# A decode attention block: a stretch of unrolled head groups put into a hardware loop with fixed tiles and register-addressed loads

## The chip, the cores and the metric

The kernel runs on one core of one Trainium2 chip. The metric is the device time of one execution in microseconds (us); several executions are timed and medians quoted. An execution under the profiler gives a span about 2 us below the timed value, since it leaves out start and end.

Names: PE is the matmul engine, DVE the vector engine, ACT the scalar engine, SP the engine that here issues nearly all DMA loads. "SPq" in a profile line is SP's instruction queue. A load is one DMA instruction; it is spread over 16 DMA engines and is done, "landed", when all 16 have reported to its semaphore (16 landing records for each load in the traces).

## The reference, cut to what matters

```python
# x (4,1,512); k_cache, v_cache (4,32,4096,128) bf16; 32 heads of 128
h = layernorm(x) * (1 + ca) + sa
q = h @ wq                                          # per head
p = softmax(einsum('bhqd,bhkd->bhqk', q, k_cache) * 128**-0.5)
o = einsum('bhqk,bhkd->bhqd', p, v_cache)
x = x + ga * (o.reshape(...) @ wo)
# ... then a small gated MLP on 4 tokens
```

Only one query token per batch row is there, so K and V (134 MB each) are read once and nearly nothing else matters: 282.7 MB are read in all.

## The kernel before

Heads are taken in 8 groups of 4, and for each of the 4 batch rows one group is a "quad": 32 quads, each with one K load and one V load of 4 MB (128 partitions of 32 KB). Everything is unrolled by Python. `kt` and `vt` are double buffers handed out by a pool.

```python
def load(cache, i, tag, parts):
    t = kvp.tile([P, NT * DH], BF16, name=tag, bufs=2)
    a = 0
    for part in parts:
        b = a + NT * DH // part
        nc.sync.dma_start(out=t[:, a:b], in_=kv_view(cache, i)[:, a:b])
        a = b
    return t.rearrange("p (n d) -> p n d", d=DH)
# ... cut ...
st["k", 0] = load_k(0)
for i in range(NQ):                        # 32 quads
    if i + 1 < NQ:
        st["k", i + 1] = load_k(i + 1)
    if quads[i][1] == 0:                   # first quad of a group
        g = quads[i][0]
        if g < G - 1:
            st["wo", g] = wk.tile([P, NH, D], BF16, name="wo_g", bufs=2)
            nc.sync.dma_start(out=st["wo", g], in_=wo_w[g])
    st["v", i] = load_v(i)
    # ... cut: the last quad's extra loads and its order of work ...
    if i > 1: diagonal(i - 2)
    scores(i, 0)                           # DVE product, then 16 PE matmuls
    if i > 1: project(i - 2)
    scores(i, 1)
    fold(i, 0); fold(i, 1)
    if i != NQ - 2: softmax(i)
    if i > 0: values(i - 1)
    if i > 1: apply(i - 2)
```

Each load reports to one of eight semaphores, taken in turn over the whole program; before a semaphore is used again, SP waits until its last load has landed.

Of the kernel before, what the change touches and what calls it, by code (L numbers as in the profile page):

```python
# [16 lines left out]
def kernel(  # L17
# [16 lines left out]
    nc = tc.nc  # L34
# [35 lines left out]
    def vslot(cols):  # L70
        return kvp.tile([P, cols], BF16, name="vt", bufs=2)

    wm = vslot(J * 6 * D)
# [3 lines left out]
    wq = vslot(J * G * GW)  # L77
# [3 lines left out]
    quads = [(g, b) for g in range(G) for b in range(B)]  # L81

    def kv_view(cache, i):
        g, b = quads[i]
        return cache[b, g * NH:(g + 1) * NH].rearrange("h (s n) d -> (h s) (n d)", s=R)

    def load(cache, i, tag, parts):
        t = kvp.tile([P, NT * DH], BF16, name=tag, bufs=2)
        a = 0
        for part in parts:  # L90
            b = a + NT * DH // part
            nc.sync.dma_start(out=t[:, a:b], in_=kv_view(cache, i)[:, a:b])  # L92
            a = b
        return t.rearrange("p (n d) -> p n d", d=DH)

    def load_k(i):
        return load(A_k_cache, i, "kt", (2, 2) if i == len(quads) - 1 else (1,))

    def load_v(i):
        return load(A_v_cache, i, "vt", (2, 4, 8, 16, 16) if i == len(quads) - 1 else (1,))  # L100

    NQ = len(quads)
# [30 lines left out]
    NB = 3  # L133
# [135 lines left out]
    with tc.tile_pool(name="psum_att", bufs=1, space=bass.MemoryType.PSUM) as psum:  # L269
        st = {}  # L270

        def scores(i, half):
            g, b = quads[i]
            kt = st["k", i][:, half * HT:(half + 1) * HT, :]
            q = qbc[:, b, g, :]
            nc.vector.tensor_tensor(  # L276
                out=kt, in0=kt, in1=q[:, None, :].to_broadcast([P, HT, DH]), op=ALU.mult,
            )
            ps = psum.tile([P, HT, DC], F32, name="s_ps", bufs=2)
            for cc in range(DH // DC):  # L280
                nc.tensor.matmul(  # L281
                    ps, lhsT=ident, rhs=kt[:, :, cc * DC:(cc + 1) * DC],
                    start=(cc == 0), stop=(cc == DH // DC - 1),
                )
            st["s", i, half] = ps

        def fold(i, half):
            if half == 0:
                st["S", i] = wk.tile([P, NT], F32, name="S", bufs=3)
            nc.vector.tensor_reduce(  # L290
                out=st["S", i][:, half * HT:(half + 1) * HT], in_=st.pop(("s", i, half)),
                axis=AX.X, op=ALU.add,
            )

        def softmax(i):
            S = st.pop(("S", i))
            mx, P4 = mxs[i % NB], P4s[i % NB]
            nc.vector.tensor_reduce(out=mx[:, 0:1], in_=S, axis=AX.X, op=ALU.max)
            mT = wk.tile([P, R], F32, name="mT", bufs=2)
            nc.vector.transpose(out=mT, in_=mx)  # L300
            hm = wk.tile([P, 1], F32, name="hm", bufs=2)
            nc.vector.tensor_reduce(out=hm, in_=mT, axis=AX.X, op=ALU.max)
            hb = wk.tile([P, R], F32, name="hb", bufs=2)
# [3 lines left out]
            nm = wk.tile([P, R], F32, name="nm", bufs=2)  # L307
            nc.vector.transpose(out=nm, in_=hb)  # L308
            E = wk.tile([P, NT], F32, name="E", bufs=2)
            rs = wk.tile([P, 1], F32, name="rs", bufs=2)  # L310
# [7 lines left out]
            rs4 = wk.tile([P, NH], F32, name="rs4", bufs=3)  # L318
            nc.vector.tensor_scalar_mul(out=rs4, in0=mask4, scalar1=rs)
            st["rs4", i] = rs4  # L320

        def zsum(i):
            zo = psum.tile([P, 2, NH], F32, name="zo_ps", bufs=2)
            st["z", i], st["o", i] = zo[:, 0], zo[:, 1]
            if i == NQ - 1:
                st["z", i] = psum_s.tile([P, NH], F32, name="small", bufs=1)
            nc.tensor.matmul(
                st["z", i], lhsT=ones_f, rhs=st.pop(("rs4", i)), start=True, stop=True,
            )

        def values(i):


            P4 = P4s[i % NB]
            zsum(i)
            po = psum_s.tile([P, 4, DH], F32, name="big", bufs=2)
            NU = NT // 16
            for u in range(NU):
                for t in range(4):
# [3 lines left out]
                        rhs=st["v", i][:, n0:n0 + 4, :],  # L343
                        start=(u == 0), stop=(u == NU - 1), tile_position=(0, 32 * t),
                    )
            osb = wk.tile([P, 4, DH], F32, name="osb", bufs=2)
            nc.scalar.copy(out=osb, in_=po)  # L347
            st["osb", i] = osb

        def diagonal(i):  # L350

            osb = st.pop(("osb", i))
            for n in range(4):
                nc.tensor.matmul(  # L354
                    st["o", i], lhsT=osb[:, n, :], rhs=sel[:, NH * n:NH * n + NH],
                    start=(n == 0), stop=(n == 3),
                )

        def values_last(i):
            P4 = P4s[i % NB]  # L360
            zsum(i)
            for n in range(NT):
                nc.tensor.matmul(  # L363
                    st["o", i], lhsT=st["v", i][:, n, :], rhs=P4[:, n, :],
# [3 lines left out]
        def project(i):  # L368
            g, b = quads[i]
            if b == 0:  # L370
                st["oT", g] = wk.tile([P, NH, B], BF16, name="oT", bufs=2)
            oT = st["oT", g]
            rz = wk.tile([P, NH], F32, name="rz", bufs=2)
            nc.vector.reciprocal(out=rz, in_=st.pop(("z", i)))
            nc.vector.tensor_tensor(  # L375
                out=oT[:, :, b], in0=st.pop(("o", i)), in1=rz, op=ALU.mult,
            )
            if i == NQ - 1:
                apply(i)

        def apply(i):
            g, b = quads[i]
            if b == B - 1:
                oT = st.pop(("oT", g))
                if g < G - 1:
                    wo_g = st.pop(("wo", g))

                    pp = psum_s.tile([P, NH, B], F32, name="small", bufs=1)
                    for r in range(NH):
                        for hl in range(NH):  # L390
                            nc.tensor.matmul(
                                pp[hl * R:(hl + 1) * R, r, :], lhsT=ident[:, r::NH],
                                rhs=oT[:, hl, :], start=True, stop=True,
                                tile_position=(0, hl * R),
                            )
                    oT = wk.tile([P, NH, B], BF16, name="oP", bufs=2)
                    nc.vector.tensor_copy(out=oT, in_=pp)  # L397
                for hl in range(NH):
                    for jo in range(J):
                        nc.tensor.matmul(  # L400
                            attn_ps[:, jo, :],
                            lhsT=(wo_g[:, hl] if g < G - 1 else wo_l[hl // 2][:, hl % 2])[
                                :, jo * P:(jo + 1) * P],
                            rhs=oT[:, hl, :],
                            start=(g == 0 and hl == 0 and jo == 0),
                            stop=(g == G - 1 and hl == NH - 1),
                            skip_group_check=True,
                        )

# [19 lines left out]
        for i in range(NQ):  # L429
            if i + 1 < NQ:  # L430
                st["k", i + 1] = load_k(i + 1)
# [144 lines left out]
```

## Time and profile before

| | |
|---|---|
| time | 667.5 us |
| SP's loads: share of the 16 DMA engines' span | 98.9% |
| PE, DVE busy | 62%, 61% |
| one 4 MB load: 8 packets of 32 KB per engine, 1.213 us each (packet records) | 9.7 us |
| K load from issue to landing, median | 26.0 us |

These lines are from the page of the kernel before: its busy table, the DMA row (busy tenths in 40 equal slices of the span) and what the DMA engines moved in each slice (GB/s), the queue table (packets, MB, share of 16 engines; q1 is SP's queue, q8 is listed there as `instruction`, read here as instruction fetches), the chain of waits by engine, one group of instructions and two groups of loads.

```profile
span 665.5 us, 6939 instructions
PE 415.7 (62%) x3024; PEld 204.6 (31%) x3024; DVE 402.6 (61%) x475; ACT 41.3 (6%) x115; POOL 4.7 (1%) x21
...
DMA  9999999999999999999999999999999999999995
GB/s 379 439 425 427 437 439 424 429 438 434 427 428 441 428 428 434 435 426 434 433 436 424 436 435 430 423 439 435 428 431 435 433 430 432 437 426 435 428 417 236
...
q1 hardware_dynamic: 12640, 282.73, 98.9%
q8 instruction: 23, 0.38, 0.2%
...
DMA 62%; PE 24%; DVE 12%; issue 0%; SPq 0%; ACT 0%; DVEq 0%
...
L276 DVE TENSOR_TENSOR kt<-kt,qbc 128x8192 bf16<-128x8192 bf16 x64 | 282.7, 4420 | 82.9 <-DMA kt<-in_A_k_cache_dram 82.9
...
kt<-in_A_k_cache_dram SPq DMA_DIRECT2D x31, 4096.0 KB, 26.0
vt<-in_A_v_cache_dram SPq DMA_DIRECT2D x31, 4096.0 KB, 33.7
```

The DMA engines are full in every slice but the last. A K load moves for 9.7 us and takes 26 us to land, so about 16 us of other loads stand ahead of it. The chain seems to give PE and DVE a third, but that is only the path by which a K load's issue is reached; the engines that move bytes never stop. So a few us of delay at SP, PE or DVE should cost nothing, as long as these 16 us of queue don't run empty.

### The profile page before, as it was taken

To read this page: it belongs to the slowest core of one execution; us is meant where nothing else is said; L and a number is where in the kernel's file an instruction comes from. 1 tells how busy PE (TensorE), PEld (TensorE's weight loads), DVE (VectorE), ACT (ScalarE), POOL (GpSimd) and SP (SyncE) were. 2 spreads that over 40 slices of the span, in tenths; PEclk is the share of its full clock that TensorE was granted. 3 is DMA by queue.
4 is the path that set the end of the run, shared out by engine and by line. 5 is a ranking of instruction groups with operands and counts; after the bars stand their busy time and mean duration, and the time that the engine had idled before them with its cause. 6 is when DMAs were issued, how large, how long until landed. Compare 5 with 4: busy or idle time off the path is not lost.

```text
span 665.5 us, 6939 instructions
## 1 busy us (share of the span) xinstructions
PE 415.7 (62%) x3024; PEld 204.6 (31%) x3024; DVE 402.6 (61%) x475; ACT 41.3 (6%) x115; POOL 4.7 (1%) x21
## 2 busy tenths in 40 slices
PE   2557776655677655676555477654657655657775
PEld 2223333222333322233222233232223322223334
DVE  2166776675556576547666456666555666655762
ACT  1200000000000000000000000000000000000002
POOL 2000000000000000000000000000000000000000
PEclk9977777668887667887667788676888766888795
DMA  9999999999999999999999999999999999999995
GB/s 379 439 425 427 437 439 424 429 438 434 427 428 441 428 428 434 435 426 434 433 436 424 436 435 430 423 439 435 428 431 435 433 430 432 437 426 435 428 417 236
DMA packets 12749, 283.17 MB, mean 426 GB/s; under 512 B 1448, under 2 KB 1968, under 8 KB 4016
## 3 DMA queue, kind: packets, MB, share of 16 engines
q1 hardware_dynamic: 12640, 282.73, 98.9%
q8 instruction: 23, 0.38, 0.2%
q14 instruction: 6, 0.05, 0.0%
q0 software_dynamic: 64, 0.00, 0.0%
q10 hardware_dynamic: 16, 0.01, 0.0%
HBM read 282.73 MB, written 0.00 MB: 425 GB/s over the span
## 4 chain that ended last, share of the span: by engine, by line
DMA 62%; PE 24%; DVE 12%; issue 0%; SPq 0%; ACT 0%; DVEq 0%
DMA kt<-in_A_k_cache_dram 58%; PE s_ps L281 24%; DVE kt L276 11%; DMA vt<-in_A_v_cache_dram 3%; DMA wout_437<-in_B_w_out_dram 1%; PE big L341 0%; DVE S L290 0%; ACT E L311 0%; SPq L92 0%; DVE P_1_109 L314 0%; DVE P_0_105 L314 0%; PE y_ps L522 0%; DVE nm L308 0%; DVE mT L300 0%; SPq L78 0%
## 5 line engine op out<-in xcount | busy, mean ns | idle before, releaser
L281 PE MATMUL s_ps<-kt,ident 128*128 128x512 bf16 x1024 | 293.5, 457 | 185.5 <-DVE kt L276 185.5
L276 DVE TENSOR_TENSOR kt<-kt,qbc 128x8192 bf16<-128x8192 bf16 x64 | 282.7, 4420 | 82.9 <-DMA kt<-in_A_k_cache_dram 82.9
L281 PEld LDWEIGHTS <-ident 128*128 128x128 bf16 x1024 | 116.4, 114 | 351.1 <-issue 229.8
L290 DVE TENSOR_REDUCE S<-s_ps 128x64 f32<-128x512 f32 x64 | 44.3, 692 | 125.5 <-PE s_ps L281 125.5
L354 PE MATMUL zo_ps<-sel,osb 128*128 128x4 f32 x248 | 33.2, 257 | 26.6 <-ACT osb L347 26.6
L311 ACT ACTIVATE E<-S,nm 128x128 f32<-128x128 f32 x32 | 12.8, 401 | 563.4 <-DVE nm L308 563.4
L354 PEld LDWEIGHTS zo_ps<-sel,osb 128*128 128x128 f32 x248 | 30.6, 194 | 38.4 <-ACT osb L347 38.4
L341 PE MATMUL big<-vt,P_0_105 128*32 128x512 bf16 x352 | 21.0, 380 | 1.5 <-DMA vt<-in_A_v_cache_dram 1.5
L341 PE MATMUL big<-vt,P_1_109 128*32 128x512 bf16 x320 | 19.1, 380 | 0.0
L341 PE MATMUL big<-vt,P_2_113 128*32 128x512 bf16 x320 | 19.1, 380 | 0.0
L347 ACT COPY osb<-big 128x512 f32<-128x512 f32 x31 | 17.6, 566 | 20.0 <-PE big L341 20.0
L215 PE MATMUL big<-vt,hbc 128*32 128x512 bf16 x128 | 9.6, 471 | 5.2 <-DMA vt<-in_A_wq_dram 5.2
L314 DVE TENSOR_TENSOR P_1_109<-E,mask_99 128x512 bf16<-128x512 f32 x11 | 7.6, 692 | 6.8 <-ACT E L311 6.8
L314 DVE TENSOR_TENSOR P_0_105<-E,mask_99 128x512 bf16<-128x512 f32 x11 | 7.6, 692 | 6.7 <-ACT E L311 6.7
L341 PEld LDWEIGHTS <-P_0_105 128*32 128x32 bf16 x352 | 8.4, 96 | 8.9 <-DMA vt<-in_A_v_cache_dram 1.6
L314 DVE TENSOR_TENSOR P_2_113<-E,mask_99 128x512 bf16<-128x512 f32 x10 | 6.9, 692 | 6.2 <-ACT E L311 6.2
L400 PE MATMUL attn_ps<-oP,wo_g 128*128 128x4 bf16 x112 | 3.8, 164 | 10.6 <-DVE oP L397 10.6
L341 PEld LDWEIGHTS <-P_1_109 128*32 128x32 bf16 x320 | 7.6, 96 | 6.7
L341 PEld LDWEIGHTS <-P_2_113 128*32 128x32 bf16 x320 | 7.6, 96 | 6.7
L375 DVE TENSOR_TENSOR oT<-zo_ps,rz 128x4 bf16<-128x4 f32 x32 | 5.4, 168 | 7.1 <-PE zo_ps L363 6.0
L215 PEld LDWEIGHTS <-hbc 128*32 128x32 bf16 x128 | 4.4, 114 | 10.3 <-issue 8.4
L308 DVE STREAM_TRANSPOSE nm<-hb 128x32 f32<-128x32 f32 x32 | 6.8, 212 | 1.1
(221 smaller groups left out, 131.1 us busy)
## 6 DMA issues: line engine op xcount, KB each, us to landing
kt<-in_A_k_cache_dram SPq DMA_DIRECT2D x31, 4096.0 KB, 26.0
vt<-in_A_v_cache_dram SPq DMA_DIRECT2D x31, 4096.0 KB, 33.7
vt<-in_A_wq_dram SPq DMA_DIRECT2D x1, 4096.0 KB, 20.4
kt<-in_A_k_cache_dram SPq DMA_DIRECT2D x2, 2048.0 KB, 24.8
wo_g<-in_A_wo_dram SPq DMA_DIRECT2D x7, 512.0 KB, 26.5
vt<-in_w_mod_dram SPq DMA_DIRECT2D x1, 3072.0 KB, 9.8
vt<-in_A_v_cache_dram SPq DMA_DIRECT2D x1, 2048.0 KB, 17.8
win_434<-in_B_w_in_dram SPq DMA_DIRECT2D x1, 1344.0 KB
```

Of the source, the lines that this page charges most:

```text
L215: nc.tensor.matmul(qp[hl * R:(hl + 1) * R, 0:n], lhsT=hbc[:, j, b, :], rhs=wv[:, g0:g0 + n, hl, :], start=(j == 0), stop=(j == J - 1), til ...
L276: nc.vector.tensor_tensor(out=kt, in0=kt, in1=q[:, None, :].to_broadcast([P, HT, DH]), op=ALU.mult,)
L281: nc.tensor.matmul(ps, lhsT=ident, rhs=kt[:, :, cc * DC:(cc + 1) * DC], start=(cc == 0), stop=(cc == DH // DC - 1),)
L290: nc.vector.tensor_reduce(out=st["S", i][:, half * HT:(half + 1) * HT], in_=st.pop(("s", i, half)), axis=AX.X, op=ALU.add,)
L308: nc.vector.transpose(out=nm, in_=hb)
L311: nc.scalar.activation(out=E, in_=S, func=AF.Exp, bias=nm[:, 0:1], scale=att_scale, accum_out=rs,)
L314: nc.vector.tensor_tensor(out=P4[:, 0:NT, :], in0=E[:, :, None].to_broadcast([P, NT, NH]), in1=mask4[:, None, :].to_broadcast([P, NT, NH]) ...
L341: nc.tensor.matmul(po[32 * t:32 * t + 32], lhsT=P4[:, n0:n0 + 8, :], rhs=st["v", i][:, n0:n0 + 4, :], start=(u == 0), stop=(u == NU - 1), ...
L347: nc.scalar.copy(out=osb, in_=po)
L354: nc.tensor.matmul(st["o", i], lhsT=osb[:, n, :], rhs=sel[:, NH * n:NH * n + NH], start=(n == 0), stop=(n == 3),)
L375: nc.vector.tensor_tensor(out=oT[:, :, b], in0=st.pop(("o", i)), in1=rz, op=ALU.mult,)
L400: nc.tensor.matmul(attn_ps[:, jo, :], lhsT=(wo_g[:, hl] if g < G - 1 else wo_l[hl // 2][:, hl % 2])[:, jo * P:(jo + 1) * P], rhs=oT[:, hl, :],
```

## The change

Its intent is a smaller program. (Two words for what follows: the jump from the end of a pass to its start is a back edge; a drain is a stretch in which SP's queue of loads runs empty.) Groups 1 to 6 run in a hardware loop, six passes of four quads; the first five quads and the last three stay unrolled. For that every buffer is one fixed tile, the softmax buffers are four, wo has one buffer in place of two, and K, V and wo addresses come from a register. The accumulator is cleared by one matmul so that all later ones accumulate.

```diff
+    kts = [kvp.tile([P, NT * DH], BF16, name=f"kt{a}", align_bytes=128) for a in range(2)]
+    vts = [kvp.tile([P, NT * DH], BF16, name=f"vt{a}", align_bytes=128) for a in range(2)]
 ... cut: all other buffers likewise ...
+    def kv_view(cache, g, b):
+        return cache[b, bass.ds(g * NH, NH)].rearrange("h (s n) d -> (h s) (n d)", s=R)
-    NB = 3
+    NB = 4
 ... cut ...
+        wo_g = wk.tile([P, NH, D], BF16, name="wo_g", align_bytes=128)
+            q = qbc[:, b, bass.ds(g, 1), :]
 ... cut ...
+        def step(g, b, first=9):
+            last = g is G - 1 and b == B - 1
+            if not last:
+                load(A_k_cache, kts[(b + 1) % 2], g + (b + 1) // B, (b + 1) % B,
+                     (2, 2) if g is G - 1 and b == B - 2 else (1,))
+            if b == 0 and first > 0:
+                nc.sync.dma_start(out=wo_g, in_=wo_w[bass.ds(g - 1, 1)])
+            load(A_v_cache, vts[b % 2], g, b, (2, 4, 8, 16, 16) if last else (1,))
 ... cut: the same order of work as before ...
+        load(A_k_cache, kts[0], 0, 0, (1,))
+        for i in range(B + 1):
+            step(i // B, i % B, i)
+        with tc.For_i(1, G - 1, 1, iteration_sync="reg_based") as g:
+            for b in range(1, B):
+                step(g, b)
+            step(g + 1, 0)
+        for b in range(1, B):
+            step(G - 1, b)
```

`iteration_sync="reg_based"` means here that the built program has no barrier between passes (in the trace SP waits on no semaphore at the loop's own line between 98 and 583 us; from 583.0 to 617.9, at the exit, it waits there on the eight of the loop); each wait compares a semaphore with a register that grows by a fixed amount per pass. The listing of the built program shows what that makes of SP's loads in a pass. Condensed (S0 to S7 are the loop's eight semaphores, n the pass from 0):

```
load 1  K    waits S0 >= 32 + 32 n   (and counts of PE, DVE)   then reports to S0
load 2  V    ...                                               S1
load 3  K    ...                                               S2
load 4  V    ...                                               S3
load 5  K    ...                                               S4
load 6  V    ...                                               S5
load 7  K    ...                                               S6
load 8  wo   ...                                               S7
load 9  V    ...                                               S0
branch back; S0 starts at 32 and gets 16 from load 1 and 16 from load 9 in each pass
```

More of the change, by code (lines that the diff above doesn't have):

```diff
@@ L67 @@
     nc.gpsimd.dma_start(out=wb_t[:, 1:2], in_=B_b_sp.rearrange("(a b) -> a b", b=1))
-    def vslot(cols):
-        return kvp.tile([P, cols], BF16, name="vt", bufs=2)
-    wm = vslot(J * 6 * D)
+    kts = [kvp.tile([P, NT * DH], BF16, name=f"kt{a}", align_bytes=128) for a in range(2)]
+    vts = [kvp.tile([P, NT * DH], BF16, name=f"vt{a}", align_bytes=128) for a in range(2)]
+    wm = vts[0][:, 0:J * 6 * D]
     nc.sync.dma_start(out=wm, in_=w_mod.rearrange("(p j) n -> p (j n)", j=J))
@@ L76, with load @@
     GW = NH * DH
-    wq = vslot(J * G * GW)
+    wq = vts[1]
     nc.sync.dma_start(out=wq, in_=A_wq.rearrange("(p j) n -> p (j n)", j=J))
     wq = wq.rearrange("p (j n) -> p j n", j=J)
-    quads = [(g, b) for g in range(G) for b in range(B)]
-    def kv_view(cache, i):
-        g, b = quads[i]
-        return cache[b, g * NH:(g + 1) * NH].rearrange("h (s n) d -> (h s) (n d)", s=R)
-    def load(cache, i, tag, parts):
-        t = kvp.tile([P, NT * DH], BF16, name=tag, bufs=2)
-        a = 0
-        for part in parts:
-            b = a + NT * DH // part
-            nc.sync.dma_start(out=t[:, a:b], in_=kv_view(cache, i)[:, a:b])
-            a = b
-        return t.rearrange("p (n d) -> p n d", d=DH)
-    def load_k(i):
-        return load(A_k_cache, i, "kt", (2, 2) if i == len(quads) - 1 else (1,))
-    def load_v(i):
-        return load(A_v_cache, i, "vt", (2, 4, 8, 16, 16) if i == len(quads) - 1 else (1,))
-    NQ = len(quads)
+    NQ = G * B
+    def kv_view(cache, g, b):
+        return cache[b, bass.ds(g * NH, NH)].rearrange("h (s n) d -> (h s) (n d)", s=R)
+    def load(cache, t, g, b, parts):
+        lo = 0
+        for part in parts:
+            hi = lo + NT * DH // part
+            nc.sync.dma_start(out=t[:, lo:hi], in_=kv_view(cache, g, b)[:, lo:hi])
+            lo = hi
     ident = consts.tile([P, P], BF16, name="ident")
@@ L269 @@
     with tc.tile_pool(name="psum_att", bufs=1, space=bass.MemoryType.PSUM) as psum:
-        st = {}
-        def scores(i, half):
-            g, b = quads[i]
-            kt = st["k", i][:, half * HT:(half + 1) * HT, :]
-            q = qbc[:, b, g, :]
+        Ss = [wk.tile([P, NT], F32, name=f"S{a}") for a in range(B)]
+        rs4s = [wk.tile([P, NH], F32, name=f"rs4_{a}") for a in range(B)]
+        Es = [wk.tile([P, NT], F32, name=f"E{a}") for a in range(2)]
+        rss = [wk.tile([P, 1], F32, name=f"rs{a}") for a in range(2)]
@@ new lines @@
+        mTs = [wk.tile([P, R], F32, name=f"mT{a}") for a in range(2)]
+        hms = [wk.tile([P, 1], F32, name=f"hm{a}") for a in range(2)]
+        hbs = [wk.tile([P, R], F32, name=f"hb{a}") for a in range(2)]
+        nms = [wk.tile([P, R], F32, name=f"nm{a}") for a in range(2)]
+        rzs = [wk.tile([P, NH], F32, name=f"rz{a}") for a in range(2)]
+        osbs = [wk.tile([P, 4, DH], F32, name=f"osb{a}") for a in range(2)]
+        oTt = wk.tile([P, NH, B], BF16, name="oTt")
+        oPt = wk.tile([P, NH, B], BF16, name="oPt")
@@ new lines @@
+        wo_g = wk.tile([P, NH, D], BF16, name="wo_g", align_bytes=128)
+        wo_l = [
+            wk.tile([P, NH // 2, D], BF16, name=f"wo_l{a}", align_bytes=128) for a in range(2)
+        ]
+        s_pss = [psum.tile([P, HT, DC], F32, name=f"s_ps{a}") for a in range(2)]
+        zos = [psum.tile([P, 2, NH], F32, name=f"zo_ps{a}") for a in range(2)]
+        bigs = [psum_s.tile([P, 4, DH], F32, name="big", bufs=2) for a in range(2)]
+        smallt = psum_s.tile([P, NH, B], F32, name="small", bufs=1)
@@ L276, in scores @@
+        busy_ps[0] = bigs[0].rearrange("p n d -> p (n d)")
+        def scores(g, b, half):
+            kt = kts[b % 2].rearrange("p (n d) -> p n d", d=DH)[:, half * HT:(half + 1) * HT, :]
+            q = qbc[:, b, bass.ds(g, 1), :]
             nc.vector.tensor_tensor(
-                out=kt, in0=kt, in1=q[:, None, :].to_broadcast([P, HT, DH]), op=ALU.mult,
+                out=kt, in0=kt, in1=q.to_broadcast([P, HT, DH]), op=ALU.mult,
             )
-            ps = psum.tile([P, HT, DC], F32, name="s_ps", bufs=2)
@@ L280, in scores, with fold @@
             for cc in range(DH // DC):
                 nc.tensor.matmul(
-                    ps, lhsT=ident, rhs=kt[:, :, cc * DC:(cc + 1) * DC],
+                    s_pss[half], lhsT=ident, rhs=kt[:, :, cc * DC:(cc + 1) * DC],
                     start=(cc == 0), stop=(cc == DH // DC - 1),
                 )
-            st["s", i, half] = ps
-        def fold(i, half):
-            if half == 0:
-                st["S", i] = wk.tile([P, NT], F32, name="S", bufs=3)
+        def fold(b, half):
@@ L290, in fold, with softmax @@
             nc.vector.tensor_reduce(
-                out=st["S", i][:, half * HT:(half + 1) * HT], in_=st.pop(("s", i, half)),
+                out=Ss[b][:, half * HT:(half + 1) * HT], in_=s_pss[half],
                 axis=AX.X, op=ALU.add,
             )
-        def softmax(i):
-            S = st.pop(("S", i))
-            mx, P4 = mxs[i % NB], P4s[i % NB]
+        def softmax(b):
+            S, mx, P4 = Ss[b], mxs[b], P4s[b]
+            mT, hm, hb, nm, E, rs = (t[b % 2] for t in (mTs, hms, hbs, nms, Es, rss))
@@ L298, in softmax @@
             nc.vector.tensor_reduce(out=mx[:, 0:1], in_=S, axis=AX.X, op=ALU.max)
-            mT = wk.tile([P, R], F32, name="mT", bufs=2)
             nc.vector.transpose(out=mT, in_=mx)
-            hm = wk.tile([P, 1], F32, name="hm", bufs=2)
             nc.vector.tensor_reduce(out=hm, in_=mT, axis=AX.X, op=ALU.max)
-            hb = wk.tile([P, R], F32, name="hb", bufs=2)
             nc.vector.tensor_scalar_mul(
@@ L306, in softmax @@
             )
-            nm = wk.tile([P, R], F32, name="nm", bufs=2)
             nc.vector.transpose(out=nm, in_=hb)
-            E = wk.tile([P, NT], F32, name="E", bufs=2)
-            rs = wk.tile([P, 1], F32, name="rs", bufs=2)
             nc.scalar.activation(
@@ L317, in softmax, with zsum, values @@
             )
-            rs4 = wk.tile([P, NH], F32, name="rs4", bufs=3)
-            nc.vector.tensor_scalar_mul(out=rs4, in0=mask4, scalar1=rs)
-            st["rs4", i] = rs4
-        def zsum(i):
-            zo = psum.tile([P, 2, NH], F32, name="zo_ps", bufs=2)
-            st["z", i], st["o", i] = zo[:, 0], zo[:, 1]
-            if i == NQ - 1:
-                st["z", i] = psum_s.tile([P, NH], F32, name="small", bufs=1)
-            nc.tensor.matmul(
-                st["z", i], lhsT=ones_f, rhs=st.pop(("rs4", i)), start=True, stop=True,
-            )
-        def values(i):
-            P4 = P4s[i % NB]
-            zsum(i)
-            po = psum_s.tile([P, 4, DH], F32, name="big", bufs=2)
+            nc.vector.tensor_scalar_mul(out=rs4s[b], in0=mask4, scalar1=rs)
+        def zsum(b, z):
+            nc.tensor.matmul(z, lhsT=ones_f, rhs=rs4s[b], start=True, stop=True)
+        def values(b):
+            P4, po = P4s[b], bigs[b % 2]
+            vt = vts[b % 2].rearrange("p (n d) -> p n d", d=DH)
+            zsum(b, zos[b % 2][:, 0])
             NU = NT // 16
@@ L342, in values @@
                         po[32 * t:32 * t + 32], lhsT=P4[:, n0:n0 + 8, :],
-                        rhs=st["v", i][:, n0:n0 + 4, :],
+                        rhs=vt[:, n0:n0 + 4, :],
                         start=(u == 0), stop=(u == NU - 1), tile_position=(0, 32 * t),
                     )
-            osb = wk.tile([P, 4, DH], F32, name="osb", bufs=2)
-            nc.scalar.copy(out=osb, in_=po)
-            st["osb", i] = osb
-        def diagonal(i):
-            osb = st.pop(("osb", i))
+            nc.scalar.copy(out=osbs[b % 2], in_=po)
@@ L353, in diagonal, with values_last @@
+        def diagonal(b):
             for n in range(4):
                 nc.tensor.matmul(
-                    st["o", i], lhsT=osb[:, n, :], rhs=sel[:, NH * n:NH * n + NH],
+                    zos[b % 2][:, 1], lhsT=osbs[b % 2][:, n, :], rhs=sel[:, NH * n:NH * n + NH],
                     start=(n == 0), stop=(n == 3),
                 )
-        def values_last(i):
-            P4 = P4s[i % NB]
-            zsum(i)
+        def values_last(b):
+            vt = vts[b % 2].rearrange("p (n d) -> p n d", d=DH)
+            zsum(b, smallt[:, 0])
@@ L362, in values_last @@
             for n in range(NT):
                 nc.tensor.matmul(
-                    st["o", i], lhsT=st["v", i][:, n, :], rhs=P4[:, n, :],
+                    zos[b % 2][:, 1], lhsT=vt[:, n, :], rhs=P4s[b][:, n, :],
                     start=(n == 0), stop=(n == NT - 1),
                 )
-        def project(i):
-            g, b = quads[i]
-            if b == 0:
-                st["oT", g] = wk.tile([P, NH, B], BF16, name="oT", bufs=2)
-            oT = st["oT", g]
-            rz = wk.tile([P, NH], F32, name="rz", bufs=2)
-            nc.vector.reciprocal(out=rz, in_=st.pop(("z", i)))
-            nc.vector.tensor_tensor(
-                out=oT[:, :, b], in0=st.pop(("o", i)), in1=rz, op=ALU.mult,
-            )
-            if i == NQ - 1:
-                apply(i)
@@ L381, in apply @@
-        def apply(i):
-            g, b = quads[i]
-            if b == B - 1:
-                oT = st.pop(("oT", g))
-                if g < G - 1:
-                    wo_g = st.pop(("wo", g))
-                    pp = psum_s.tile([P, NH, B], F32, name="small", bufs=1)
-                    for r in range(NH):
-                        for hl in range(NH):
-                            nc.tensor.matmul(
-                                pp[hl * R:(hl + 1) * R, r, :], lhsT=ident[:, r::NH],
-                                rhs=oT[:, hl, :], start=True, stop=True,
-                                tile_position=(0, hl * R),
-                            )
-                    oT = wk.tile([P, NH, B], BF16, name="oP", bufs=2)
-                    nc.vector.tensor_copy(out=oT, in_=pp)
-                for hl in range(NH):
-                    for jo in range(J):
-                        nc.tensor.matmul(
-                            attn_ps[:, jo, :],
-                            lhsT=(wo_g[:, hl] if g < G - 1 else wo_l[hl // 2][:, hl % 2])[
-                                :, jo * P:(jo + 1) * P],
-                            rhs=oT[:, hl, :],
-                            start=(g == 0 and hl == 0 and jo == 0),
-                            stop=(g == G - 1 and hl == NH - 1),
-                            skip_group_check=True,
-                        )
@@ new lines, in project, with apply @@
+        def project(b, z=None):
+            zo, rz = zos[b % 2], rzs[b % 2]
+            nc.vector.reciprocal(out=rz, in_=zo[:, 0] if z is None else z)
+            nc.vector.tensor_tensor(out=oTt[:, :, b], in0=zo[:, 1], in1=rz, op=ALU.mult)
+        def apply(last=False):
+            oT, ws = oTt, [wo_l[hl // 2][:, hl % 2] for hl in range(NH)]
+            if not last:
+                for r in range(NH):
+                    for hl in range(NH):
+                        nc.tensor.matmul(
+                            smallt[hl * R:(hl + 1) * R, r, :], lhsT=ident[:, r::NH],
+                            rhs=oT[:, hl, :], start=True, stop=True, tile_position=(0, hl * R),
+                        )
+                nc.vector.tensor_copy(out=oPt, in_=smallt)
+                oT, ws = oPt, [wo_g[:, hl] for hl in range(NH)]
+            for hl in range(NH):
+                for jo in range(J):
+                    nc.tensor.matmul(
+                        attn_ps[:, jo, :], lhsT=ws[hl][:, jo * P:(jo + 1) * P], rhs=oT[:, hl, :],
+                        start=False, stop=(last and hl == NH - 1), skip_group_check=True,
+                    )
@@ L416 @@
         win = [
-            persist.tile([P, j1 - j0, F], BF16, name=f"win{a}") for a, (j0, j1) in enumerate(WJS)
+            persist.tile([P, j1 - j0, F], BF16, name=f"win{a}", align_bytes=128)
+            for a, (j0, j1) in enumerate(WJS)
         ]
@@ L424 @@
         wout = [
-            persist.tile([P, j1 - j0, D], BF16, name=f"wout{a}") for a, (j0, j1) in enumerate(JFS)
-        ]
-        wo_l = [wk.tile([P, NH // 2, D], BF16, name=f"wo_l{a}", bufs=1) for a in range(2)]
-        st["k", 0] = load_k(0)
-        for i in range(NQ):
-            if i + 1 < NQ:
-                st["k", i + 1] = load_k(i + 1)
-            if quads[i][1] == 0:
-                g = quads[i][0]
-                if g < G - 1:
-                    st["wo", g] = wk.tile([P, NH, D], BF16, name="wo_g", bufs=2)
-                    nc.sync.dma_start(out=st["wo", g], in_=wo_w[g])
-            st["v", i] = load_v(i)
-            if i == NQ - 1:
+            persist.tile([P, j1 - j0, D], BF16, name=f"wout{a}", align_bytes=128)
+            for a, (j0, j1) in enumerate(JFS)
+        ]
+        nc.tensor.matmul(
+            attn_ps.rearrange("p j b -> p (j b)"), lhsT=ident, rhs=wide[:, 0:J * B],
+            start=True, stop=False, skip_group_check=True,
+        )
+        def step(g, b, first=9):
+            last = g is G - 1 and b == B - 1
+            if not last:
+                load(A_k_cache, kts[(b + 1) % 2], g + (b + 1) // B, (b + 1) % B,
[3 more added lines that the diff above has]
+            load(A_v_cache, vts[b % 2], g, b, (2, 4, 8, 16, 16) if last else (1,))
+            if last:
                 for a in range(2):
@@ L446 @@
                     nc.sync.dma_start(out=wout[a], in_=wout_v[a])
-            if i > 1:
-                diagonal(i - 2)
-            if i == NQ - 1:
+            b1, b2 = (b - 1) % B, (b - 2) % B
+            if first > 1:
+                diagonal(b2)
+            if last:
                 keep_busy(4)
-            scores(i, 0)
-            if i > 1:
-                project(i - 2)
-            scores(i, 1)
-            if i == NQ - 1:
-                softmax(i - 1)
-            fold(i, 0)
-            fold(i, 1)
-            if i != NQ - 2:
-                softmax(i)
-            if i > 0:
-                values(i - 1)
-            if i > 1:
-                apply(i - 2)
-        diagonal(NQ - 2)
-        project(NQ - 2)
-        values_last(NQ - 1)
-        project(NQ - 1)
+            scores(g, b, 0)
+            if first > 1:
+                project(b2)
+            scores(g, b, 1)
+            if last:
+                softmax(b1)
+            fold(b, 0)
+            fold(b, 1)
+            if not (g is G - 1 and b == B - 2):
+                softmax(b)
+            if first > 0:
+                values(b1)
+            if first > 1 and b2 == B - 1:
+                apply()
+        load(A_k_cache, kts[0], 0, 0, (1,))
[7 more added lines that the diff above has]
+            step(G - 1, b)
+        diagonal(B - 2)
+        project(B - 2)
+        values_last(B - 1)
+        project(B - 1, smallt[:, 0])
+        apply(True)
     with tc.tile_pool(name="post", bufs=1) as post, \
```

## The prediction

> **What bounds the kernel now.** The DMA engines. The page's queue table gives the SP queue 98.9% of the 16 engines' span; the row of 40 slices shows DMA at 9 tenths or more in all but the last. A 4 MB K or V load is eight 32 KB packets per engine of 1.213 us each (packet records), 9.7 us. PE (62%) and DVE (61%) have room. The chain of waits repeats: DVE product 4.4 us, PE scores 9.3 us, then a K load, about 26 us from issue to landing, because two loads stand ahead of it. That queue (some 16 us) hides whatever SP, PE, DVE and ACT do between loads.
>
> **What the change does.** Bytes, packets and the engines' work per quad stay. Register arithmetic, branches and changed instruction fetches lie off the bottleneck: a few us per pass vanish in the 16 us of queue. [...]
>
> **Where it costs.** The order of the built program, with its waits, shows two places where the queue must run empty.
> 1. A pass issues nine loads (four K, four V, one wo) on eight DMA semaphores; its first K load and last V load share one. Before its first load each later pass waits until that semaphore has all counts of the pass before, so for the V load issued just before the branch, the last in the queue. The unrolled kernel reuses eight semaphores too, but always eight loads later. Five back edges (the first pass finds its count satisfied).
> 2. At the loop's exit SP waits for all its loads, and all engines pass a barrier, before the next K load.
>
> **Cost of a drain.** At the trace's start, with an empty queue, the first load was issued at 0.75 us; its first packet began 1.25 us later, the first 16 packets took mostly 1.5 to 1.9 us in place of 0.91, and it landed 2.7 us later than its packets at full rate account for. [...] My estimate: 2.5 to 3.3 us a back edge, 4 to 5 us for the exit: 5 x 2.9 + 4.5 = 19 us, all on the critical path. Against it about 1 us, from fewer fetches and because the engines, whose landings spread from 2 us to 5 us apart over the run before (landing records), are brought together again.
>
> **Prediction.** 667.5 + 19 - 1 = 685.5 us; range 679 to 693. Faster by over 2%: 0.01. Within 2% (up to 680.9): 0.19. Slower by over 2%: 0.80.
>
> **What would show it.** SP's waits: five waits of a pass's first K load for a V landing, 15 to 35 us each; gaps of 2 to 4 us in DMA, one about every 80 us from about 210 us on, the longest at the exit near 620 us; the SP queue's share falls to 95 to 97%; DVE product still near 4.4 us.
>
> **What would make it wrong.** A wait value I misread, so that passes overlap: then only the exit costs, near 672. A restart below 2 us: within 2%. Register-addressed loads slower to generate, a DVE product slowed by its register-addressed operand, or instruction fetches that outlast the queue: over 693.

5 x 2.9 + 4.5 = 19 us, less 1 us, on 667.5 us gives 685.5. The 2.9 us is the estimate from the restart at the trace's start alone; the 4.5 us for the exit and the credit of 1 us are estimates too. What the credit was put down to was measured afterwards: 11 fetch packets in place of 23, and landings 0.55 us apart after the first drain in place of 2.08 before it.

Two figures under "Cost of a drain" are 0.25 us too large, because packet times and issue times were read on two clocks. On one clock the first packet begins 1.00 us after the first issue (1.75 against 0.75 us). The first load lands 9.8 us after its issue, and eight packets of 0.912 us on each engine make 7.3 of that, so 2.5 us are lost and not 2.7. The argument doesn't depend on it.

## More of the kernel before

SP's timeline shows the rhythm (start, duration, what was issued): one K and one V load every 18 to 22 us.

```profile
174.13 0.33 SPq L92 DMA_DIRECT2D kt<-in_A_k_cache_dram  x1
...
192.34 0.33 SPq L92 DMA_DIRECT2D kt<-in_A_k_cache_dram  x1
194.31 0.33 SPq L92 DMA_DIRECT2D vt<-in_A_v_cache_dram  x1
212.24 0.33 SPq L92 DMA_DIRECT2D kt<-in_A_k_cache_dram  x1
```

Three stretches of the table by windows, for later comparison (stretch and its length; busy us of each engine and instruction counts; granted clock; DMA share; GB/s):

```profile
206.00:213.00 7.00, 7.00 (x44) 3.22 (x45) 2.84 (x4) 0.00 (x0) 0.00 (x0) 0.89 1.01 435
288.00:295.00 7.00, 5.54 (x67) 2.92 (x65) 3.37 (x10) 0.96 (x3) 0.00 (x0) 1.00 1.01 433
...
615.00:622.00 7.00, 3.44 (x9) 1.24 (x9) 6.96 (x4) 0.00 (x0) 0.00 (x0) 0.50 0.97 415
```

## The result, and the profile after

The changed kernel takes 685.4 us (684.7 to 686.0, four runs) against 667.5 us: ratio 1.0267, 95% interval 1.0249 to 1.0285, slower. Ratios here are the mean time of one kernel's runs over that of the other's runs of the same rounds, so not quite the ratio of the medians quoted.

The page of the changed kernel, the same parts as before except the chain of waits:

```profile
span 683.6 us, 7735 instructions
PE 409.2 (60%) x3025; PEld 202.5 (30%) x3025; DVE 404.1 (59%) x475; ACT 41.1 (6%) x115; POOL 5.2 (1%) x23
...
DMA  8999999999998999999998999989999899997996
GB/s 371 433 437 437 431 430 429 430 429 429 431 431 347 429 429 429 399 399 429 429 431 366 429 431 441 437 349 441 433 435 437 360 433 431 431 429 328 427 416 254
...
q1 hardware_dynamic: 12640, 282.73, 96.8%
q8 instruction: 11, 0.18, 0.1%
...
L286 DVE TENSOR_TENSOR kt_76<-kt_76,qbc 128x8192 bf16<-128x8192 bf16 x32 | 141.5, 4424 | 62.1 <-DMA kt_76<-in_A_k_cache_dram 62.1
...
kt_76<-in_A_k_cache_dram SPq DMA_DIRECT2D x16, 4096.0 KB, 24.3
vt_78<-in_A_v_cache_dram SPq DMA_DIRECT2D x16, 4096.0 KB, 33.9
```

Bytes and packets are the same. The register-addressed DVE product takes 4424 ns against 4420. The row of GB/s has six dips in the loop's part and at its end (347, 399 in two slices, 366, 349, 360, 328); in the kernel before, no slice but the first and the last lies below 417. The DMA row is too coarse to show all six. Instruction fetches halved: 11 packets, 0.18 MB.

SP's timeline around the first back edge, and the lines of SP's waits that name a V load inside the loop and at its exit (total us, times, longest us):

```profile
172.87 0.33 SPq L91 DMA_DIRECT2D kt_77<-in_A_k_cache_dram  x1
...
175.16 0.33 SPq L91 DMA_DIRECT2D vt_78<-in_A_v_cache_dram  x1
208.94 0.34 SPq L91 DMA_DIRECT2D kt_76<-in_A_k_cache_dram  x1
209.66 0.33 SPq L91 DMA_DIRECT2D vt_79<-in_A_v_cache_dram  x1
```

```profile
SPq L91 <- DMA vt_78<-in_A_v_cache_dram: 85.1, 5, 17.7
...
SPq L447 <- DMA vt_78<-in_A_v_cache_dram: 21.5, 1, 21.5
```

Between 175.16 and 208.94 us SP issues nothing (the V load issued at 175.16 has its last landing at 208.74, 0.20 us before the next issue), where the kernel before issued at 192.34 and 194.31. It has five waits of a K load for a V landing, 17 us each on average, and one more at the exit (L447 is the loop). The table by windows at the first two back edges and at the exit:

```profile
206.00:213.00 7.00, 7.00 (x74) 3.49 (x72) 3.34 (x8) 0.00 (x0) 0.00 (x0) 1.00 0.53 183
288.00:295.00 7.00, 6.99 (x73) 3.58 (x72) 3.23 (x8) 0.00 (x0) 0.00 (x0) 1.00 0.72 276
...
615.00:622.00 7.00, 1.84 (x8) 1.81 (x9) 3.54 (x1) 0.00 (x0) 0.00 (x0) 0.50 0.47 164
```

At the two back edges the DMA share falls from 1.01 to 0.53 and 0.72 in 7 us, while PE is fully busy: it isn't PE that waits. At the exit it falls from 0.97 to 0.47.

From the packet records one can ask when each multiple of 8.39 MB (one quad) had been moved, and how much later than in the kernel before:

```
lateness against the kernel before, us, just before and just after each of the six places
quad                 10 > 11      14 > 15      18 > 19      22 > 23      26 > 27      30 > 31     33
changed kernel      0.4 > 3.8    3.7 > 6.6    6.4 > 9.2    9.0 > 11.7  11.4 > 14.4  14.2 > 18.5   18.8
```

The time is lost in six steps: 3.4, 2.9, 2.8, 2.7, 3.0 us at the back edges and 4.3 us around the exit, 19.1 us in all. Between the steps 1.0 us is won back.

One drain in detail, the second: the last packet ends at 290.26 us, its engine's count lands at 290.58, SP issues at 290.78, the first new packet starts at 291.76, the sixteenth engine starts at 292.42, and these first packets take 1.78 us on average in place of 1.213.

### The profile page after: what moved, and what is told of

Same layout as the page of the kernel before. It is cut to its first block, busy times and chain, and to the rows that moved or that the text cites. A ratio compares the mean times of both kernels' runs of the same rounds, so it can differ in the third digit from the quotient of the medians.

```text
span 683.6 us, 7735 instructions
## 1 busy us (share of the span) xinstructions
PE 409.2 (60%) x3025; PEld 202.5 (30%) x3025; DVE 404.1 (59%) x475; ACT 41.1 (6%) x115; POOL 5.2 (1%) x23
## 3 DMA queue, kind: packets, MB, share of 16 engines
q1 hardware_dynamic: 12640, 282.73, 96.8%
## 5 line engine op out<-in xcount | busy, mean ns | idle before, releaser
L290 PEld LDWEIGHTS <-ident 128*128 128x128 bf16 x1024 | 115.0, 113 | 358.5 <-issue 194.1
L286 DVE TENSOR_TENSOR kt_76<-kt_76,qbc 128x8192 bf16<-128x8192 bf16 x32 | 141.5, 4424 | 62.1 <-DMA kt_76<-in_A_k_cache_dram 62.1
L286 DVE TENSOR_TENSOR kt_77<-kt_77,qbc 128x8192 bf16<-128x8192 bf16 x32 | 141.5, 4424 | 45.2 <-DMA kt_77<-in_A_k_cache_dram 30.2
L290 PE MATMUL s_ps_469<-kt_76,ident 128*128 128x512 bf16 x256 | 88.3, 521 | 104.5 <-DVE kt_76 L286 104.5
L290 PE MATMUL s_ps_469<-kt_77,ident 128*128 128x512 bf16 x256 | 89.7, 527 | 90.8 <-DVE kt_77 L286 50.5
L290 PE MATMUL s_ps_470<-kt_77,ident 128*128 128x512 bf16 x256 | 57.9, 379 | 1.0 <-DVE kt_77 L286 1.0
L290 PE MATMUL s_ps_470<-kt_76,ident 128*128 128x512 bf16 x256 | 57.9, 379 | 0.0
L343 PE MATMUL zo_ps_472<-sel,osb_463 128*128 128x4 f32 x120 | 16.5, 261 | 33.0 <-PEq L560 16.6
L343 PEld LDWEIGHTS zo_ps_472<-sel,osb_463 128*128 128x128 f32 x120 | 15.3, 200 | 40.2 <-issue 25.3
L343 PE MATMUL zo_ps_471<-sel,osb_462 128*128 128x4 f32 x128 | 16.9, 256 | 10.3 <-ACT osb_462 L338 10.3
L343 PEld LDWEIGHTS zo_ps_471<-sel,osb_462 128*128 128x128 f32 x128 | 15.7, 193 | 14.7 <-ACT osb_462 L338 14.7
L296 DVE TENSOR_REDUCE S_440<-s_ps_470 128x64 f32<-128x512 f32 x8 | 5.5, 692 | 22.1 <-PE s_ps_470 L290 22.1
L296 DVE TENSOR_REDUCE S_442<-s_ps_470 128x64 f32<-128x512 f32 x8 | 5.5, 692 | 22.1 <-PE s_ps_470 L290 22.1
L296 DVE TENSOR_REDUCE S_441<-s_ps_470 128x64 f32<-128x512 f32 x8 | 5.5, 692 | 21.7 <-PE s_ps_470 L290 21.7
L296 DVE TENSOR_REDUCE S_443<-s_ps_470 128x64 f32<-128x512 f32 x8 | 5.5, 692 | 19.9 <-PE s_ps_470 L290 19.9
L333 PE MATMUL big<-vt_78,P_2_115 128*32 128x512 bf16 x256 | 15.3, 380 | 0.0
L333 PE MATMUL big<-vt_78,P_0_107 128*32 128x512 bf16 x256 | 15.3, 380 | 0.0
L333 PE MATMUL big<-vt_79,P_1_111 128*32 128x512 bf16 x256 | 15.3, 380 | 0.0
L333 PE MATMUL big<-vt_79,P_3_119 128*32 128x512 bf16 x224 | 13.4, 380 | 0.0
L311 ACT ACTIVATE E_449<-S_441,nm_459 128x128 f32<-128x128 f32 x8 | 3.2, 401 | 161.5 <-DVE nm_459 L310 161.5
L311 ACT ACTIVATE E_448<-S_442,nm_458 128x128 f32<-128x128 f32 x8 | 3.2, 401 | 156.6 <-DVE nm_458 L310 156.6
L206 PE MATMUL big<-vt_79,hbc 128*32 128x512 bf16 x128 | 8.7, 438 | 4.9 <-DMA vt_79<-in_A_wq_dram 4.9
```

The lines of the kernel that those rows point to most:

```text
L206: nc.tensor.matmul(qp[hl * R:(hl + 1) * R, 0:n], lhsT=hbc[:, j, b, :], rhs=wv[:, g0:g0 + n, hl, :], start=(j == 0), stop=(j == J - 1), til ...
L286: nc.vector.tensor_tensor(out=kt, in0=kt, in1=q.to_broadcast([P, HT, DH]), op=ALU.mult,)
L290: nc.tensor.matmul(s_pss[half], lhsT=ident, rhs=kt[:, :, cc * DC:(cc + 1) * DC], start=(cc == 0), stop=(cc == DH // DC - 1),)
L296: nc.vector.tensor_reduce(out=Ss[b][:, half * HT:(half + 1) * HT], in_=s_pss[half], axis=AX.X, op=ALU.add,)
L311: nc.scalar.activation(out=E, in_=S, func=AF.Exp, bias=nm[:, 0:1], scale=att_scale, accum_out=rs,)
L333: nc.tensor.matmul(po[32 * t:32 * t + 32], lhsT=P4[:, n0:n0 + 8, :], rhs=vt[:, n0:n0 + 4, :], start=(u == 0), stop=(u == NU - 1), tile_pos ...
```

## The experiments

Theory A, from the prediction: nine loads on eight semaphores make load 1 of a pass wait for load 9 of the pass before, which is the newest in the queue; the queue runs empty, and restarting costs about 2.7 us. Rival B: the loop's machinery costs (branch, refetched instructions, register arithmetic, register-addressed loads). Rival C: the fixed tiles and the single wo buffer cost.

### One load more per pass

```diff
-                nc.sync.dma_start(out=wo_g, in_=wo_w[bass.ds(g - 1, 1)])
+                for a in range(2):
+                    nc.sync.dma_start(
+                        out=wo_g[:, a * NH // 2:(a + 1) * NH // 2],
+                        in_=wo_w[bass.ds(g - 1, 1), :, a * NH // 2:(a + 1) * NH // 2],
+                    )
```

> Only edit: the wo load of a pass is issued in two halves, so a pass has ten loads on eight semaphores in place of nine. The pass's first K load then shares its semaphore with the second wo half (which lands one V load earlier), and the second load with the last V. Theory A (the five back edges cost because the ninth load and the first share a semaphore, so the queue drains): the five drains of about 2.7 us vanish, only the exit's drain of about 4 us stays, 685.4 - 13.5 = 672 us (669 to 674); SP still waits at a back edge, but for the wo half, and the DMA row shows one gap, at the exit. Rival B (the loop's own machinery costs: branch, refetch of instructions, register-addressed loads, register arithmetic): nothing of it changes and one more load is issued, 685 to 687. Rival C (fixed tiles and the single wo buffer cost): 685.

Measured: 671.7 us (ratio to the kernel before 1.0063, 1.0046 to 1.0080). With the same loop, the same branches and registers, and one instruction more, the loop loses 13.7 us of its 17.9. Its page (DMA row and queue), SP's waits and its timeline:

```profile
DMA  9999999999999999999999999999999999998996
...
q1 hardware_dynamic: 13648, 282.73, 98.5%
```

```profile
SPq L91 <- DMA wo_g<-in_A_wo_dram: 35.1, 5, 7.7
```

```profile
199.49 0.34 SPq L91 DMA_DIRECT2D kt<-in_A_k_cache_dram  x1
209.16 0.33 SPq L91 DMA_DIRECT2D vt<-in_A_v_cache_dram  x1
```

The five waits are still there, but for the wo half, 7 us each in place of 17, and the K load goes out at 199.49, 9.5 us earlier than in the changed kernel. One V load is then still in the queue, so nothing empties. Rival B falls: its cost was untouched.

### Finer loads, but the count wrong again

```diff
-                     (2, 2) if g is G - 1 and b == B - 2 else (1,))
+                     (2, 2))
-            load(A_v_cache, vts[b % 2], g, b, (2, 4, 8, 16, 16) if last else (1,))
+            load(A_v_cache, vts[b % 2], g, b, (2, 4, 8, 16, 16) if last else (2, 2))
```

> Only edit: every K and V load in two halves, wo whole: seventeen loads a pass. The pass's first load shares its semaphore with the seventeenth, the last V half, as in the changed kernel, so this is the control for the splitting itself. Theory A: the five drains stay, 685 us (681 to 689), five waits of the first K half for the last V landing. Theory that smaller loads by themselves help (finer issue, more in the queue): near 672. Rival B: 685 to 689.

Measured: 687.2 us (1.0295). All engines stand still at the same six places, for 1.5 to 1.6 us at each back edge and 2.1 us at the exit. Splitting doesn't help by itself; with one load over a multiple of eight (nine, 685.4 us, and seventeen, 687.2) the back edges drain, with two over (ten, 671.7, and eighteen, 671.3, the next run) they don't. No other remainder was run.

### Two groups per pass

```diff
-        with tc.For_i(1, G - 1, 1, iteration_sync="reg_based") as g:
-            for b in range(1, B):
-                step(g, b)
-            step(g + 1, 0)
+        with tc.For_i(1, G - 1, 2, iteration_sync="reg_based") as g:
+            for h in range(2):
+                for b in range(1, B):
+                    step(g + h, b)
+                step(g + h + 1, 0)
```

> Two groups per pass, three passes: eighteen loads a pass on eight semaphores. The first load of a pass shares its semaphore with the seventeenth (wo) and the second with the eighteenth (V), so by theory A no back edge drains although nothing is split: exit only, 671.5 us (669 to 674). Rival B (each back edge costs by itself, 2.7 us): two back edges and the exit, 677 us.

Measured: 671.3 us (1.0055). Two back edges are taken and they cost nothing. So eighteen loads are as good as ten (671.3 against 671.7 us).

### No loop at all

```diff
-        with tc.For_i(1, G - 1, 1, iteration_sync="reg_based") as g:
+        for g in range(1, G - 1):
```

> Only edit: the hardware loop replaced by a Python loop; fixed tiles, four softmax buffers and the single wo buffer of the changed kernel stay, all addresses constant. Theory A and rival B: 667.5 us, within 2 us of the kernel before. Rival C (fixed tiles, the single wo buffer): near 685.

Measured: 669.2 us (1.0026, 1.0009 to 1.0042). Rival C falls as an explanation of the 18 us, but 1.7 us are real; they are taken up below.

### The drain without the loop

The unrolled kernel gets seven loads of 4 bytes at each of the six boundaries:

```diff
+        tiny = wk.tile([1, 8, 64], BF16, name="tiny", align_bytes=128)
-        for g in range(1, G - 1):
+        for g in range(1, G):
+            if g > 1:
+                for a in range(7):
+                    nc.sync.dma_start(out=tiny[:, a, 0:2], in_=B_w_in[0:1, 2 * a:2 * a + 2])
+            if g == G - 1:
+                break
```

> The unrolled kernel with fixed tiles plus seven loads of 4 bytes at each of the six places where the loop has a back edge or its exit. No loop, no branch, no register address, no barrier: the seven small loads only turn the eight semaphores on, so that the next K load shares its semaphore with the V load just issued and must wait for its landing. Theory A: six drains of about 2.7 us, 667.5 + 16 = 683.5 us (680 to 687), six gaps of 2 to 3 us in DMA. Rival B: 668 us, as seven loads of 4 bytes move nothing.

Measured: 689.9 us (1.0333), 20.7 us over the unrolled kernel: 3.4 us a boundary. The effect is there without any loop, but larger than expected; the time lies above the range of theory A. So one of the seven was left out:

```diff
-                for a in range(7):
+                for a in range(6):
```

> The kernel with seven small loads at each of six boundaries, with one of the seven left out (six loads of 4 bytes). The next K load then shares its semaphore with the wo load, which lands one V load before the end of the queue, so nothing drains. It also tells why seven cost 3.4 us a boundary where the loop's back edges cost 2.7. Theory A: 669.2 us plus what 36 small loads cost in a full queue, at most 4 us: 669 to 673; one small load fewer per boundary saves some 17 to 20 us. Rival (the small loads themselves cost 3.4 us a boundary): 669.2 + 6/7 x 20.7 = 687 us.

Measured: 669.7 us (1.0036). Thirty-six loads of 4 bytes cost about half a us (0.4 by the medians, 0.7 against the kernel before in the same rounds); the other six cost 20 us. The same window in both kernels, seven small loads first, then six:

```profile
288.00:295.00 7.00, 7.00 (x44) 3.20 (x45) 2.81 (x3) 0.00 (x0) 0.00 (x0) 0.88 0.63 222
```

```profile
288.00:295.00 7.00, 6.16 (x70) 3.20 (x68) 2.76 (x8) 0.82 (x3) 0.00 (x0) 1.00 1.01 429
```

Why 3.4 us and not 2.7? The landing records show the likely reason. At the second drain the 16 engines of the last V load finish between 289.5 and 291.3 us, 1.8 us apart; in the changed kernel between 290.1 and 290.6, 0.5 us apart. The drain waits for the slowest engine: SP's next K load goes out at 291.37 us. The unrolled program keeps fetching instructions (about one 16 KB packet of 1.0 us per 30 us, on one engine each; in the kernel before 23 packets of 0.88 to 0.97 us); the changed kernel's loop fetches none between 155 and 605 us. That the fetches make the whole difference was not tested by a run.

### Passes counted

The loop runs one pass or three, and the remaining groups are unrolled behind it:

```diff
-        with tc.For_i(1, G - 1, 1, iteration_sync="reg_based") as g:
+        with tc.For_i(1, 2, 1, iteration_sync="reg_based") as g:
 ...
+        for g in range(2, G - 1):
+            for b in range(1, B):
+                step(g, b)
+            step(g + 1, 0)
```

> The loop runs one pass (group 1), groups 2 to 6 are unrolled behind it: no back edge is taken, the loop's exit with its barrier comes once, near 209 us. Theory A: the exit alone, 667.5 + 4 = 671.5 us (669.5 to 673.5). If the exit cost no more than a back edge: 670.

> The loop runs three passes (groups 1 to 3), the rest unrolled: two back edges and the exit. Theory A: 671.5 + 2 x 2.7 = 677 us (675 to 679), so that one, three and six passes lie on a line of 2.7 us a pass. Rival (a fixed cost of having the loop at all): the same as with one pass or with six.

Measured: 674.0 us with one pass (1.0091) and 678.1 with three (1.0154). Against the right base, the unrolled kernel with the same tiles (669.2), the exit costs 4.8 us. One pass lies 0.5 us above the range I gave, because I had taken 667.5 as its base. From one pass to three is 2.1 us per back edge, from three to six 2.4. That is under the 2.7 to 3.4 us of the steps, at least in part because in the lateness record of the changed kernel each pass wins back 0.1 to 0.3 us. That this comes from the instruction fetches which a pass saves was not tested by a run. These runs show no fixed cost of having a loop besides the exit.

### A barrier in place of register waits

```diff
-        with tc.For_i(1, G - 1, 1, iteration_sync="reg_based") as g:
+        with tc.For_i(1, G - 1, 1, iteration_sync="barrier") as g:
```

> The same loop with the full barrier as iteration synchronisation in place of register-based waits. The built program then has SP wait for all its loads and all engines meet at the loop's entry, at five back edges and at the exit: seven drains of the exit's kind. Theory A (what costs is the empty queue, and an exit costs about 4 us): 667.5 + 7 x 4 = 695 us (690 to 702).

Measured: 691.7 us (1.0368). SP's waits count six drains, not seven:

```profile
SPq L447 <- DMA vt<-in_A_v_cache_dram: 189.0, 6, 33.2
```

I had read a wait at the loop's entry into the listing; none is paid there. So the time lies in the range with one drain fewer than I counted. At the five back edges the barrier costs about 1.5 us more than the drain alone (4.1 to 4.9 us in the lateness record, the gap with no engine at work 3.1 us in place of 1.6). Its exit is the cheaper one, 2.9 us with a gap of 1.8 against 4.3 with 2.1 in the changed kernel; why was not looked into.

### The 1.7 us of the fixed tiles

In the packet records of the unrolled kernel the median 32 KB packet into `kt1` and `vt1` took about 1.216 us, in the kernel before 1.213 everywhere. The addresses differ: all four K and V tiles of the kernel before start at a multiple of 256 bytes, in the unrolled one three of four don't.

```diff
-name=f"kt{a}", align_bytes=128
+name=f"kt{a}", align_bytes=256
-name=f"vt{a}", align_bytes=128
+name=f"vt{a}", align_bytes=256
```

> The unrolled kernel with fixed tiles, its K and V tiles aligned to 256 bytes in place of 128. Open is the 1.7 us that the fixed tiles cost without any loop: the median 32 KB packet into kt1 and vt1 took about 1.216 us there, into kt0 and vt0 1.213, and 1.213 everywhere in the kernel before, whose four tiles all start on a 256-byte boundary (three of four did not in the unrolled one). If the placement costs: all packets 1.213 us and 667.5 us (667.2 to 668.2). If something else of the fixed tiles costs (the single wo buffer, order of the tiles): 669.2 again. A doubt beforehand: kt0 was off the boundary too, and its packets were not slower.

> The loop with ten loads per pass and K and V tiles aligned to 256 bytes. If placement costs 1.7 us in the unrolled kernel, 671.7 - 1.5 = 670 us here; else 671.7. It would be the best version with a loop; it beats the kernel before only if the exit's drain (4 us) were paid back, which nothing suggests.

> The changed kernel with nothing but its K and V tiles aligned to 256 bytes in place of 128. If the placement and the drains add up, 685.4 - 1.7 = 683.7 us (683 to 684.7), packets of 1.213 us in kt1 and vt1 too. If the placement is hidden by the drains: 685.4.

Measured: unrolled 667.55 us against 667.64 before (0.9999, 0.9985 to 1.0012); ten loads 670.0 us (1.0034); the changed kernel with nothing else altered 683.0 against 667.3 of its rounds (1.0234). In the unrolled and the ten-load kernel, packets of 1.213 us from the 1st to the 99th percentile are back. So the placement is the whole of the 1.7 us without a loop (no other tile's offset from a 256-byte boundary changed), and it adds to the drains. How it costs is less clear. Summed over the packets of an engine, the longer ones make only about 0.9 of the 1.7 us. In the loop, the six steps of the lateness record come to 17.2 us with aligned tiles against 19.1, so there most of the gain of 2.2 us lies in the drains. `kt0` was off the boundary too and was not slower (1.213 us). So no run shows how the placement costs, and the rule behind it stays open.

No version beats the kernel before. The best loop (670.0 us) still pays the exit: in the lateness record it is 1.0 us ahead of the kernel before at quad 30 and 3.7 us behind at quad 31.

## Why the prediction was right

The forecast was 685.5 us, the result 685.4. Point by point:

- **The bound.** Right. DMA was full before (98.9%), and what was lost where it stood still came out in the time: 19.1 us in six steps, 1.0 us won back between them, 17.9 us more in the medians.
- **What vanishes in the slack.** Right. `two_groups` and `ten_loads` keep branches, registers and register-addressed loads and cost only the exit (671.3 and 671.7 us). The wo buffer (`unrolled_a256`, 667.55 against 667.64 us) and the DVE product (4424 against 4420 ns) cost nothing.
- **Five back edges by the shared semaphore.** Right, and shown twice: one load more in the loop takes 13.7 us away, one small load fewer in the unrolled kernel takes 20 us away. No run here tried to do without the wait.
- **Size of a drain.** 2.9 us forecast, 2.7 to 3.4 measured. The restart at the trace's start (2.5 us, read as 2.7) was a fair stand-in: there the first packet began 1.00 us after its issue, in the drain above 0.98.
- **The exit.** 4 to 5 us forecast; 4.3 in the lateness record, 4.8 by `pass1`, 4.7 in `ten_loads_a256`. Landing intervals give the drain itself 3.2 us (12.9 in place of 9.7). Most of the rest falls before it: the first 16 KB instruction fetch after the loop's passes begins at 604.9 us, and the last engine, 0.2 us behind the fifteenth in the load that landed before it, is 1.0 us behind in the next loads, the drained one among them. The drain waits for that engine (its count lands at 617.76 us, SP's next load goes out at 618.48). No run took the fetch away.
- **The small credit of 1 us.** The weakest step, right in the sum by luck. The loop did win back 1.0 us between the drains, but I hadn't seen that the new tile addresses cost time: 1.7 us in the unrolled kernel, 2.2 us in the loop. Without that the kernel comes out at 683.0 (`after_a256`).
- **Signs in the profile.** Five waits: yes, 17 us each, at the low end of the 15 to 35 given. Queue share 96.8%: in the range. Gaps: with no engine at work they are 1.5 to 1.6 us, and 2.1 at the exit, not 2 to 4; the rest of a drain is engines that start late and first packets of 1.8 us.

## What to carry to other kernels

Where a loop is DMA bound, as here (98.9%), count the loads of one pass against the semaphores they take in turn: with nine and with seventeen loads on eight, the first load of the next pass fell on the semaphore of the newest load and each back edge emptied the queue (2.7 to 3.4 us each with nine); one load more, or two groups per pass, mended it (671.7 and 671.3 us in place of 685.4). Look for the loop's exit too, where SP waited for everything once and which cost 4.3 to 4.8 us; no version with a loop avoided it. When tiles are fixed anew, compare their addresses and the packet times before crediting anything else: here they were 1.7 us.

## What else the traces show

- In the drain shown above, 0.32 us passed from the last packet's end to the landing of its count, 0.20 us more to SP's next issue, 0.98 us from there to the first packet, and the first packets took 0.57 us longer than later ones: by these records the start was the larger part. The steps at the back edges are 2.7 to 3.4 us in all.
- The changed kernel ran without one 16 KB fetch between 155 and 605 us, a stretch with all five taken branches in it, and fetches fell from 23 to 11 packets.
- In the kernel before each 16 KB fetch took about 0.9 us of one engine's time, and the landings of one load spread from 2 us apart early in the run to 5 us apart at its end; in the loop the spread fell from 2.1 to 0.5 us at the first drain and stayed at 0.5 to 0.9 us until the fetch at 604.9 us. In the kernel before, steps in the spread came with single fetches: from 2.2 to 3.3 us at the fetch at 253.5 us, from 3.4 to 4.8 at the one at 503.2.
